# Splitting the softmax division, moving the key scale and taking a sigmoid for two sequences, in an attention and gated convolution kernel whose order is written out

## The chip, the cores and the metric

The kernel runs on one core of one Trainium2 chip. A core has five engines that each run their own list of instructions in order: TensorE (PE, matrix products, with its weight loads shown apart as PEld), VectorE (DVE), ScalarE (ACT, which evaluates functions such as exp from a table that has to be loaded), GpSimd (POOL) and SyncE (SP, which here only issues transfers). Semaphores make one engine wait for another. The metric is the device time of one execution in microseconds (us), the median of the runs shown.

## The reference

Eight sequences with eight heads of 64 channels and 576 positions each. Keys and values are averaged over blocks of 8 positions, so each head has 72 of them. After the attention comes a feed-forward part with a convolution along the sequence as its gate.

```python
k_p = k.reshape(B, H, 72, 8, D).mean(axis=3)
v_p = v.reshape(B, H, 72, 8, D).mean(axis=3)
scores = (1 / sqrt(64)) * q @ k_p^T
scores = scores - max(scores, axis=-1)
attn = exp(scores) / (sum(exp(scores)) + 1e-09)
x = (attn @ v_p), heads side by side          # (8, 576, 512)
h = relu(x @ w_in)                            # 512 -> 1024
conv_out[s] = sum over k of conv_w[k] * h[s + k - 1]   # 3 taps, per channel
out = (h * sigmoid(conv_out)) @ w_out         # 1024 -> 512, f32
```

## The kernel before, in words

**Tiles and stages.** The sequences go through attention in four groups of two: g0 is sequences 0 and 1, g3 is 6 and 7. A group has 1152 rows of queries, cut into tiles (g, t) of up to 128 rows, 37 tiles in all; a tile has all eight heads. A tile goes through these steps: scores on PE (`att_scores`, L563, its products at L582 and L595), the maximum of each head on DVE (`att_max`, L608), the subtraction of it (`att_shift`; on DVE at L620, for g0 on PE at L628), exp on ACT (`att_exp`, L646), the turn of the exponentials (on PE with a copy at L671 for g0 and g1, by a transposing DMA on SP at L666 for g2 and g3), the product with the values on PE (`att_values`, L682), which also gives the sum of the exponentials in one more column per head, the division (`att_divide`, L691), and the turn of the result x (PE with a copy at L722, or DMA at L706). The division is two DVE instructions behind one another: the reciprocal of the 8 sums of each row (L695) and one product of 128 x 512 that takes it broadcast along each head (L697). They are one operation in the graph, so nothing can come between them.

**The keys.** They are loaded either raw, and then pooled by a product with a matrix of ones (`clear_pool_matrix`, L341; `prep_k`, L401), or as heads, added up on DVE (`pool_pair`) and then picked apart by a product with parts of the identity (`build_pick`, L371; `turn_pair`, L441; `turn_keys`, L463). The sums are not divided by 8. Together with the reference's 1/8 this is made good by `scale=1/64` in exp (L646) alone.

**The feed-forward part** runs by sequence. `ffn_in` (PE, L727) fills 8 blocks of 128 channels x 576 positions, and `ffn_relu` (ACT, L736) takes them out of PSUM with a scale of 0.5. The gate is worked out in halves of four blocks, (b, f4), in one of two ways. Ten of the sixteen are convolved on PE (`ffn_conv`, L889) with diagonal matrices; a tanh on ACT (`ffn_tanh`, L914) takes the result out of PSUM; every second block has its two halves of 64 partitions swapped, so it goes to a buffer `tg`; `ffn_gate` adds 1 on DVE, to the unswapped blocks in one instruction (L925) and to the swapped ones in two that also swap back (L927); `ffn_times` (L935) multiplies with h. The other six, named in `TAPS` ((4,1), (5,0), (5,1), (6,0), (6,1), (7,0)), are done by taps: one tap on ACT (L862), two on DVE (L864), tanh on ACT (L869), and then `ffn_tap_gate` adds 1 (L875) and multiplies with h (L876). Since sigmoid(y) = (1 + tanh(y/2))/2, the 0.5 of relu is the outer half. `ffn_out` (PE, L943) is the last product; its result is copied out of PSUM by ACT or DVE (L954) to a buffer `osb`, for the last group to a "late" buffer (the memory of the query buffers `qp`), and stored (L966).

**What sets the order.** Every step is put into a graph by `add` (in `add_att` L1193, `add_ffn` L1246, `add_out` L1334) with its engine or a choice of two, its predecessors and the ring buffers that it takes. Three tables written out in the class `Graph` then decide everything: `ORDER` (1034 entries: the number of a step times two, plus one for the second of its two engines; -1 is a `fill`, a matmul without use on a scratch tile, L399, of which there are 17), `FORMS` (which of two shapes the scores take) and `PLACES` (which buffer or PSUM slot each step gets). An engine runs its steps in this order. Large loads are issued on POOL's queue, raw loads, transposing DMAs and most stores on SP's, some late stores on ACT's.

Of the kernel before, what the change touches and what calls it, by code (L numbers as in the profile page):

```python
# [9 lines left out]
BF16 = mybir.dt.bfloat16  # L10
AX = mybir.AxisListType
OP = mybir.AluOpType
# [21 lines left out]
class Graph:  # L34
# [35 lines left out]
    ORDER = (  # L70
# [107 lines left out]
def kernel(  # L178
# [23 lines left out]
    KW = 2 * Sp  # L202
    SLOTS = 24
    NJ = 5
    KP = NJ * P

    groups = [[0, 1], [2, 3], [4, 5], [6, 7]]
    where = {b: (g, i) for g, bs in enumerate(groups) for i, b in enumerate(bs)}
# [50 lines left out]
    graph = Graph(rings)  # L259
    add = graph.add  # L260

    def shift_by_dve(g, t):
        return (g, t) not in Graph.SHIFT_PE

# [1152 lines left out]
```

## Time and profile before

| what | value |
|---|---|
| runs | 217.02, 217.79, 217.13 us; median 217.13 |
| profiled execution | 216.5 us from its first to its last instruction |
| busy | PE 201.9, DVE 193.2, ACT 162.7, POOL 41.5 us |
| mean granted TensorE clock | 0.992 |
| transfers | HBM read 32.52 MB, written 9.44 MB |

The profile is of one execution. Its page gives each engine's busy time, the same in 40 equal slices (a digit is a tenth), the chain of work that ended last, followed back from the end, and the costliest groups of instructions: line, engine, operation, output <- input with shapes, count | busy us, mean ns of one | idle time of the engine just before them and what ended it. The trace behind it can be asked for single stretches and for the instructions in order of time: start, duration, engine, line, operation; a row with "x2" joins two that follow one another.

### The profile page before, as it was taken

The page shows a single profiled execution, that of the slowest core. Times are in us where ns is not written, and L with a number is a line of the kernel's source. Part 1 is how long each engine was busy: PE and PEld are TensorE (multiplying, and loading weights), DVE is VectorE, ACT ScalarE, POOL GpSimd, SP SyncE. Part 2 cuts the span into 40 slices and gives each one's busy share as a digit, 9 for nine tenths or more (in the row PEclk, how much of TensorE's full clock was granted, in tenths as well). Part 3 has the DMA queues.
Part 4 walks back from the last instruction along what each step waited for, and adds up shares of the span by engine and source line. Part 5 has one row for each costly group of instructions (what it writes and reads, how often), then busy time and mean ns, then how long its engine had stood idle before and what let it go on. Part 6 is the DMA issues. An engine that isn't in the chain of part 4 may idle for free.

```text
span 216.5 us, 6617 instructions
## 1 busy us (share of the span) xinstructions
PE 201.9 (93%) x2753; PEld 137.0 (63%) x2753; DVE 193.2 (89%) x334; ACT 162.7 (75%) x278; POOL 41.5 (19%) x78
## 2 busy tenths in 40 slices
PE   7599999969999999999999899989999999999992
PEld 3557778855788776766776675665656666654451
DVE  7598989999999999999999799999899999998621
ACT  2548885896998887787497594878979999997420
POOL 8644330050052101000000030002201210370000
PEclk9799999999999999999999999999999999999999
DMA  6999999999999999969687634576347745602685
GB/s 210 227 207 209 206 207 208 210 205 206 207 205 206 154 153 179 158 164 165 131 111 100 136 74 89 58 156 148 78 104 153 158 100 123 145 0 51 169 242 171
DMA packets 48833, 33.46 MB, mean 155 GB/s; under 512 B 28300, under 2 KB 43812, under 8 KB 48804
## 3 DMA queue, kind: packets, MB, share of 16 engines
q0 software_dynamic: 15216, 15.40, 43.5%
q1 hardware_dynamic: 32512, 16.13, 36.6%
q10 hardware_dynamic: 1076, 1.52, 2.5%
q8 instruction: 21, 0.34, 0.7%
q14 instruction: 8, 0.07, 0.1%
HBM read 32.52 MB, written 9.44 MB: 194 GB/s over the span
## 4 chain that ended last, share of the span: by engine, by line
PE 45%; DVE 34%; issue 6%; ACT 6%; DMA 5%; SPq 2%; DVEq 0%
PE psum L943 20%; PE psum L727 16%; DVE negm L608 7%; DVE x L697 6%; DVE sd L620 4%; DVE gT L935 4%; DMA hT<-in_k_dram 3%; DVE v L486 3%; DVE gT L927 3%; PE psum L889 2%; DMA out_dram<-osb 2%; DVE r L695 2%; PE psum L682 2%; ACT e L646 2%; DVE gT L925 1%
## 5 line engine op out<-in xcount | busy, mean ns | idle before, releaser
L727 PE MATMUL psum<-xT,w_in_sb 128*128 128x288 bf16 x512 | 74.1, 286 | 2.2 <-DMA xT<-x 1.1
L943 PE MATMUL psum<-w_out_sb,gT 128*128 128x512 bf16 (+1 forms) x296 | 69.5, 374 | 0.7 <-DVE gT L935 0.6
L727 PEld LDWEIGHTS <-w_in_sb 128*128 128x128 bf16 x512 | 47.9, 98 | 19.1 <-issue 2.0
L736 ACT ACTIVATE hT<-psum 128x576 bf16<-128x576 f32 x64 | 40.3, 650 | 14.0 <-PE psum L727 13.4
L943 PEld LDWEIGHTS <-gT 128*128 128x128 bf16 x296 | 27.3, 98 | 26.5 <-issue 0.9
L864 DVE SCALAR_TENSOR_TENSOR tg<-hT,convw,tg 128x576 f32<-128x576 bf16 x48 | 37.6, 815 | 0.5
L608 DVE TENSOR_REDUCE negm<-psum 128x8 f32<-128x576 f32 (+2 forms) x37 | 27.5, 752 | 2.3 <-PE psum L582 1.6
L697 DVE TENSOR_TENSOR x<-psum,r 128x512 bf16<-128x512 f32 (+1 forms) x37 | 25.6, 691 | 1.4
L811 POOL COPY hT<-hT 128x126 bf16<-128x126 bf16 x16 | 7.5, 467 | 97.6 <-ACT hT L736 80.1
L620 DVE TENSOR_TENSOR sd<-psum,negm 128x576 f32<-128x576 f32 x27 | 20.2, 753 | 0.5
L682 PE MATMUL psum<-vm,eT 128*128 128x130 bf16 (+5 forms) x240 | 18.9, 222 | 1.1 <-DVE x L697 0.7
L646 ACT ACTIVATE e<-sd 128x576 bf16<-128x576 f32 x27 | 18.2, 685 | 1.3 <-DVE sd L620 1.1
L954 ACT COPY osb<-psum 128x512 f32<-128x512 f32 x27 | 15.7, 585 | 4.4 <-PE psum L943 4.2
L889 PE MATMUL psum<-hT,dw 64*64 64x288 bf16 (+2 forms) x608 | 18.7, 261 | 0.1
L682 PEld LDWEIGHTS <-eT 128*128 128x128 bf16 (+1 forms) x240 | 15.3, 100 | 5.4 <-DMA eT<-e 1.2
L862 ACT ACTIVATE tg<-hT,convw 128x576 f32<-128x576 bf16 x24 | 18.1, 772 | 0.1
L889 PEld LDWEIGHTS <-dw 64*64 64x64 bf16 x608 | 14.8, 107 | 4.6 <-issue 3.7
L869 ACT ACTIVATE gT<-tg 128x576 bf16<-128x576 f32 x24 | 16.3, 683 | 0.7 <-DVE tg L864 0.5
L914 ACT ACTIVATE gT<-psum 128x576 bf16<-128x576 f32 x20 | 12.9, 651 | 3.9 <-PE psum L889 2.7
L914 ACT ACTIVATE tg<-psum 128x576 bf16<-128x576 f32 x20 | 13.0, 652 | 2.6 <-PE psum L889 1.4
L935 DVE TENSOR_TENSOR gT<-gT,hT 128x2304 bf16<-128x2304 bf16 x10 | 13.5, 1352 | 0.1
L486 DVE TENSOR_TENSOR v<-v 128x1280 bf16<-128x1280 bf16 (+2 forms) x24 | 13.0, 540 | 0.2
(84 smaller groups left out, 234.2 us busy)
## 6 DMA issues: line engine op xcount, KB each, us to landing
out_dram<-osb SPq DMA_DIRECT2D x54, 128.0 KB, 2.4
v<-in_v_dram POOLq DMA_DIRECT2D x8, 512.0 KB, 13.1
qp<-in_q_dram POOLq DMA_DIRECT2D x7, 576.0 KB, 14.4
kk<-in_k_dram POOLq DMA_DIRECT2D x3, 1152.0 KB, 14.6
out_dram<-qp ACTq DMA_DIRECT2D x10, 128.0 KB, 2.7
hT<-in_k_dram SPq DMA_DIRECT2D x2, 576.0 KB, 5.0
w_in_sb<-in_moe_w_in_dram POOLq DMA_DIRECT2D x2, 512.0 KB, 14.2
w_out_sb<-in_moe_w_out_dram POOLq DMA_DIRECT2D x1, 1024.0 KB, 24.7
```

Source lines behind the costliest of these rows:

```text
L608: nc.vector.tensor_reduce(out=a["m"][0:rows], in_=a["s"][0:rows, :, 0:2 * KW].rearrange("p a (h s) -> p a h s", s=Sp), axis=AX.X, op=OP.ma ...
L620: nc.vector.tensor_tensor(out=a["d"][0:rows], in0=a["s"][0:rows, :, 0:2 * KW].rearrange("p a (h s) -> p a h s", s=Sp), in1=a["m"][0:rows]. ...
L646: nc.scalar.activation(out=dst, in_=src, func=ACT.Exp, scale=1.0 / (POOL * 8.0),)
L682: nc.tensor.matmul(out=a["o"][lo:hi, h // 4, (h % 4) * (D + 1):(h % 4 + x1 - x0) * (D + 1)], lhsT=a["eT"][:, j, lo:hi], rhs=buf("vm", b)[: ...
L697: nc.vector.tensor_tensor(out=a["x"][0:rows].rearrange("p (a h d) -> p a h d", a=2, d=D), in0=ov[:, :, :, 0:D], in1=r[0:rows].unsqueeze(3) ...
L727: nc.tensor.matmul(out=banks(ps)[:, j, 0:SC], lhsT=w_in_block(dc, fb), rhs=buf("xT", g)[:, dc, i * S + j * SC:i * S + (j + 1) * SC], start ...
L736: nc.scalar.activation(out=h_of(b)[:, fb].rearrange("p (a s) -> p a s", a=2), in_=banks(ps)[:, :, 0:SC], func=ACT.Relu, scale=0.5,)
L864: nc.vector.scalar_tensor_tensor(out=acc, in0=h, scalar=w, in1=acc, op0=OP.mult, op1=OP.add)
L889: nc.tensor.matmul(out=banks(pss[r ^ c])[c * D:(c + 1) * D, j, lo:hi], lhsT=dw[r * D:(r + 1) * D, tap * n_fb + fb, :], rhs=hT[r * D:(r + 1 ...
L914: nc.scalar.activation(out=t.rearrange("p (a s) -> p a s", a=2), in_=banks(ps)[:, :, 0:SC], func=ACT.Tanh, scale=0.5,)
L935: nc.vector.tensor_tensor(out=gate, in0=gate, in1=h_of(b)[:, four], op=OP.mult)
L943: nc.tensor.matmul(out=bank(ps)[0:rows, columns], lhsT=buf("gT", g)[:, fb, t * P:t * P + rows], rhs=w_out_sb[:, fb, columns], start=(fb == 0),
```

## The change

It has five parts.

1. The division is two steps of the graph, `att_invert` (the reciprocal, on DVE) and `att_divide`, which has a choice: the product on DVE as before, or eight activations on ACT of 128 x 64 each, with the reciprocal as scale. In the new order 4 of the 37 tiles are divided on ACT: (2, 5), (2, 6), (3, 1) and (3, 7). Of the others, 19 have the product right behind the reciprocal on DVE, and 14 have something else between them.
2. The scale 1/64 is in the keys: in the pooling matrix, and in `ident_k`, a scaled copy of the identity (one more DVE instruction). exp has no scale.
3. For (6, 0), (6, 1), (7, 0) and (7, 1), listed in `SIG`, relu has scale 1 and the gate is a sigmoid instead of a tanh, so the "+1" falls away: three instructions of L875's kind and one of L925's; the two swapping instructions of (7, 1) are plain copies. In these and all other halves by taps the product with h is a step of its own, `ffn_times`. All exponentials stand ahead of the first sigmoid, and ACT loads one more table there.
4. The "late" output buffers wait for the query turns of sequences 4 to 7, where before they waited for those of 7 alone.
5. `ORDER` (1097 entries, 40 fills), `FORMS` and `PLACES` are new. 12 fills, where 14 were, stand ahead of the first other matmul, and 28, where 3 were, later. Some copies go to the other engine: DVE has three more copies to `osb`, two fewer of x, two more small and one more large of keys; one more copy of the late outputs stands ahead of DVE's last gate.

`EIGHT` is empty, so the branches on it never run. The diff, cut to its core:

```diff
 class Graph:
+    EIGHT = ()
+    SIG = ((6, 0), (6, 1), (7, 0), (7, 1))
-    ORDER = (0, 10, 12, 24, 16, -1, 4, 44, -1, 28, 8, -1, 36, ...)
+    ORDER = (0, 12, 10, 24, 16, 4, 44, 28, 8, 36, 14, 32, 46, ...)
...
+    KSCALE = 1.0 / (POOL * 8.0)
...
     def clear_pool_matrix():
-        nc.vector.memset(pm[0:TB, :, 0:Sp], 1.0)
+        nc.vector.memset(pm[0:TB, :, 0:Sp], KSCALE)
...
     def build_pick():
+        nc.vector.tensor_scalar(out=ident_k, in0=ident, scalar1=KSCALE, scalar2=None, op0=OP.mult)
...
     def att_exp(g, t):
...
             func=ACT.Exp,
-            scale=1.0 / (POOL * 8.0),
         )
...
-    def att_divide(g, t):
+    def att_invert(g, t):
+        nc.vector.reciprocal(out=buf("r", g, t)[0:rows_of(g, t)], in_=att_heads(g, t)[:, :, :, D])
+
+    def att_divide(g, t, engine):
         a, rows = att[g, t], rows_of(g, t)
-        ov = a["o"][0:rows, :, 0:4 * (D + 1)].rearrange("p a (h d) -> p a h d", d=D + 1)
-        r = buf("r", g, t)
-        nc.vector.reciprocal(out=r[0:rows], in_=ov[:, :, :, D])
+        ov, r = att_heads(g, t), buf("r", g, t)
         a["x"] = buf("x", g, t)
+        if engine == "ACT":
+            for n in range(H):
+                nc.scalar.activation(
+                    out=a["x"][0:rows, n * D:(n + 1) * D],
+                    in_=ov[:, n // 4, n % 4, 0:D],
+                    func=ACT.Identity,
+                    scale=r[0:rows, n // 4, n % 4:n % 4 + 1],
+                )
+            return
         nc.vector.tensor_tensor(
...
     def ffn_relu(b, fb, ps):
...
-            scale=0.5,
+            scale=1.0 if (b, fb // 4) in Graph.SIG else 0.5,
...
+    def squash(b, fb):
+        return ACT.Sigmoid if (b, fb // 4) in Graph.SIG else ACT.Tanh
...
     def ffn_tap_gate(b, f4):
...
         nc.vector.tensor_scalar(out=gate, in0=gate, scalar1=1.0, scalar2=None, op0=OP.add)
-        nc.vector.tensor_tensor(out=gate, in0=gate, in1=h_of(b)[:, four], op=OP.mult)
...
     def ffn_gate(b, f4):
...
+        if (b, f4) in Graph.SIG:
+            for r in range(2):
+                nc.vector.tensor_copy(out=gate[r * D:(r + 1) * D, 1], in_=tg[(1 - r) * D:(2 - r) * D])
+            return
...
-        o = add(dve(0.2, 0.69), key, lambda: att_divide(g, t), after=[o], uses=[x, rr, big])
+        o = add({"DVE": 0.115}, key, lambda: att_invert(g, t), after=[o], uses=[rr, big])
+        o = add({"DVE": 0.61, "ACT": 0.82}, key, None, after=[o], uses=[x, rr, big])
+        o.emit = lambda o=o: att_divide(g, t, o.engine)
...
-            gated = add(dve(0.78, 1.39), w, lambda f4=f4: ffn_tap_gate(b, f4), after=tanh, uses=[htok[b], gtok[g]])
+            need = tanh
+            if (b, f4) not in Graph.SIG:
+                need = [add(dve(0.78), w, lambda f4=f4: ffn_tap_gate(b, f4), after=tanh, uses=[gtok[g]])]
+            gated = add(dve(1.39), w, lambda f4=f4: ffn_times(b, f4), after=need, uses=[htok[b], gtok[g]])
...
-            osb, free = (token("late", g, t), qdone[7, 0]) if g == 3 else (token("osb", g, t), [])
+            osb, free = (token("late", g, t), [x for n in range(4, B) for x in qdone[n, 0]]) if g == 3 else (token("osb", g, t), [])
...
+    late = [o for part, o in squashed if part in Graph.SIG]
+    for o in late:
+        for e in exps:
+            e.next.append((o, True))
+            o.left += 1
```

More of the change, by code (lines that the diff above doesn't have):

```diff
@@ L640, in att_exp @@
         e = a["e"] = buf("e", g, t)
+        if by_head(g, t):
+            for n in range(H):
+                r, k = n // 4, n % 4
+                at = (k // 2 * 4 + r * 2 + k % 2 if a["by_rows"] else n) * Sp
+                nc.scalar.activation(
+                    out=e[0:rows, at:at + Sp],
+                    in_=a["s"][0:rows, r, k * Sp:(k + 1) * Sp],
+                    func=ACT.Exp,
+                    bias=a["m"][0:rows, r, k:k + 1],
+                )
+            return
         src = a["d"][0:rows].rearrange("p a h s -> p a (h s)") if shift_by_dve(g, t) else a["s"][0:rows, :, 0:2 * KW]
@@ L868, in ffn_tap_tanh @@
         gate = buf("gT", g)[:, fb, i * S:(i + 1) * S].rearrange("p (a s) -> p a s", a=2)
-        nc.scalar.activation(out=gate, in_=acc_of(b, fb, ps), func=ACT.Tanh, scale=0.5)
+        nc.scalar.activation(out=gate, in_=acc_of(b, fb, ps), func=squash(b, fb), scale=0.5)
     def ffn_tap_gate(b, f4):
         g, i = where[b]
-        four = slice(4 * f4, 4 * f4 + 4)
-        gate = buf("gT", g)[:, four, i * S:(i + 1) * S]
+        gate = buf("gT", g)[:, 4 * f4:4 * f4 + 4, i * S:(i + 1) * S]
         nc.vector.tensor_scalar(out=gate, in0=gate, scalar1=1.0, scalar2=None, op0=OP.add)
-        nc.vector.tensor_tensor(out=gate, in0=gate, in1=h_of(b)[:, four], op=OP.mult)
     def ffn_conv(b, f2, pss):
@@ L1209, in add_att @@
         o = add(dve(0.75), key, lambda: att_max(g, t), after=[o], uses=[ng, s])
-        if shift_by_dve(g, t):
+        if by_head(g, t):
+            o = add({"ACT": 0.9}, key, lambda: att_exp(g, t), after=[o], uses=[e, s, ng, lim])
+            exps.append(o)
+        elif shift_by_dve(g, t):
             sd = token("sd", g, t)
@@ L1325, in add_ffn @@
                                                    uses=[cb] + (tg if fb % 2 and tg else [gtok[g]])))
+                squashed.append(((b, f4), tanh[f4][-1]))
             if f2 % 2 and cross:
[L1327 removed]
+                need = tanh[f4]
+                if (b, f4) not in Graph.SIG:
+                    need = [add(dve(0.78), w + 6 * f2 + Graph.GATE, lambda f4=f4: ffn_tap_gate(b, f4), after=tanh[f4], uses=[gtok[g]])]
+                gated = add(dve(1.39), w + 6 * f2 + Graph.GATE, lambda f4=f4: ffn_times(b, f4), after=need, uses=[htok[b], gtok[g]])
                 gdone.setdefault(b, []).append(gated)
```

26 lines of the change are left out of this document (19 added, 7 removed), and 142 rows, old and new, of tables (ORDER, PLACES).

## The prediction

> **What bounds the kernel now.** I read the page's busy totals and its slices first, to see which engines could be the bound and whether that changes on the way.
>
> ```profile
> PE 201.9 (93%) x2753; PEld 137.0 (63%) x2753; DVE 193.2 (89%) x334; ACT 162.7 (75%) x278; POOL 41.5 (19%) x78
> ...
> PE   7599999969999999999999899989999999999992
> ...
> DVE  7598989999999999999999799999899999998621
> ACT  2548885896998887787497594878979999997420
> ```
>
> TensorE (PE) and VectorE (DVE) are both near full through the middle, ScalarE (ACT) only in the last third.  Next, the chain of work that ended last:
>
> ```profile
> PE 45%; DVE 34%; issue 6%; ACT 6%; DMA 5%; SPq 2%; DVEq 0%
> ```
>
> Two engines share the path, so I asked where each rules, with a table of long stretches (columns: length, then busy time of PE, PE's weight loads, DVE, ACT and POOL, clock, DMA share, GB/s) and one of stretches of 6 us:
>
> ```profile
> 24.00:150.00 126.00, 120.03 (x1982) 87.45 (x1982) 120.93 (x209) 99.19 (x171) 17.40 (x29) 1.00 0.95 159
> 151.30:198.20 46.90, 46.90 (x354) 28.20 (x353) 44.76 (x61) 43.77 (x75) 10.29 (x20) 1.00 0.48 106
> 12.00:72.00 60.00, 55.78 (x1033) 42.68 (x1033) 56.74 (x105) 48.88 (x84) 14.32 (x20) 1.00 1.23 207
> ```
>
> ```profile
> 6.00:12.00 6.00, 4.03 (x84) 3.81 (x88) 3.25 (x13) 3.21 (x6) 4.27 (x10) 0.72 1.19 213
> ...
> 114.00:120.00 6.00, 4.77 (x103) 3.34 (x91) 5.88 (x12) 4.15 (x7) 0.00 (x0) 1.00 0.81 112
> 120.00:126.00 6.00, 5.98 (x91) 4.67 (x92) 4.47 (x10) 4.65 (x8) 0.52 (x2) 1.00 0.49 105
> ```
>
> Up to 150 us PE and DVE wait for one another in turn: PE is idle for 126 − 120.03 = 6.0 us, DVE for 5.1. Since attention alternates between them (max, shift and divide on DVE between three PE steps), what DVE saves there lets PE start sooner, up to PE's 6.0 us. From 151.3 on PE never stops, so there a shorter DVE gives nothing by itself: PE ends earlier only by what it brought along. The end shows it:
>
> ```profile
> 198.30 0.76 DVE L875 TENSOR_SCALAR gT<-gT 128x2304 bf16<-128x2304 bf16 x1 [0.89 <-ACT gT L869]
> 199.10 1.36 DVE L876 TENSOR_TENSOR gT<-gT,hT 128x2304 bf16<-128x2304 bf16 x1
> 200.38 0.45 DVE L925 TENSOR_SCALAR gT<-gT 128x1152 bf16<-128x1152 bf16 x1
> 200.84 0.92 DVE L927 TENSOR_SCALAR gT<-tg 64x1152 bf16<-64x1152 bf16 x2
> 201.80 1.36 DVE L935 TENSOR_TENSOR gT<-gT,hT 128x2304 bf16<-128x2304 bf16 x1
> ...
> 212.28 0.42 DVE L954 COPY qp<-psum 128x256 f32<-128x256 f32 x1 [0.46 <-PE psum L943]
> ```
>
> ```profile
> 199.03 13.21 PE L943 MATMUL psum<-w_out_sb,gT 128*128 128x512 bf16 x68
> ```
>
> The last gate is done at 203.16; PE streams the output product without a hole until 212.24, 68 matmuls in 13.21 us.
>
> **The change part by part.** Counts are from both programs' instruction orders, durations from these groups:
>
> ```profile
> L697 DVE TENSOR_TENSOR x<-psum,r 128x512 bf16<-128x512 f32 x35 | 24.2, 692 | 1.3
> ...
> L954 ACT COPY osb<-psum 128x512 f32<-128x512 f32 x27 | 15.7, 585 | 4.4 <-PE psum L943 4.2
> ...
> L875 DVE TENSOR_SCALAR gT<-gT 128x2304 bf16<-128x2304 bf16 x6 | 4.6, 772 | 0.9 <-ACT gT L869 0.9
> ...
> L954 DVE COPY qp<-psum 128x512 f32<-128x512 f32 x3 | 2.1, 689 | 6.0 <-PE psum L943 6.0
> ...
> L722 DVE COPY xT<-psum 128x512 bf16<-128x512 bf16 x4 | 1.6, 415 | 0.0
> ...
> L479 ACT CAST kT<-psum 128x576 bf16<-128x576 f32 x2 | 1.2, 642 | 0.2 <-PE psum L468 0.2
> ...
> L431 ACT CAST kT<-psum 64x288 bf16<-64x288 f32 x2 | 0.8, 394 | 0.0
> ...
> L431 DVE CAST kT<-psum 64x144 bf16<-64x144 f32 x2 | 0.6, 312 | 2.6 <-PE psum L406 2.6
> L431 ACT CAST kT<-psum 64x144 bf16<-64x144 f32 x2 | 0.5, 270 | 1.1 <-DVE kT L431 1.1
> ```
>
> *DVE, by durations, up to the last gate.* Off: four divides 4 × 0.69 = 2.77; the "+1" of three sigmoid gates by taps 3 × 0.77 = 2.31; the "+1" of gate (7, 1) 0.45 (its two swapped halves become plain copies of the same shape, which I leave at 0.46); two turned copies of x 2 × 0.415 = 0.83. On: three output copies that were ACT's 3 × 0.69 = 2.07, one more output copy that now stands ahead of the last gate 0.69, two small kT casts 2 × 0.31 = 0.62, one kT copy of 128 x 576 that DVE did not do before (between the 0.31 cast and ACT's 0.64 I take 0.6, bounds 0.3 to 0.8), one eT copy 0.4, the scaled identity 0.15. Sum: −6.36 + 4.53 = −1.8 us.
>
> *DVE, by neighbours.* The split lets other work stand between reciprocal and product.
>
> ```profile
> 143.79 0.20 DVE L695 RECIPROCAL r<-psum 128x8 f32<-128x8 f32 x1
> 144.02 0.69 DVE L697 TENSOR_TENSOR x<-psum,r 128x512 bf16<-128x512 f32 x1
> 144.63 0.81 DVE L864 SCALAR_TENSOR_TENSOR tg<-hT,convw,tg 128x576 f32<-128x576 bf16 x1
> ```
>
> The product, which needs the reciprocal, starts 0.03 after its end; the tap behind it, which needs neither, 0.08 before the product's end. A dependent neighbour so costs 0.11 us. Over all of DVE's list (divides, taps, gates, pooling) such neighbours fall from 74 to 62: 12 × 0.11 = −1.3 (bounds 0 and −1.5). DVE in all: −3.1 us. By position: the new order has 1 to 1.5 us *more* DVE work ahead of sequence 0's gates (at 47 us), is even near 88, 1.5 ahead near 107, 2.5 near 145, 3.1 at the last gate.
>
> [...]
>
> *ACT.* Four tiles are divided by 8 activations of 128 x 64 each. The trace has no 64-column one; from 270 ns at 144 columns and 394 at 288 a line falls to 0.20 us at 64, a scale by pointer may add 0.1, and neighbours overlap.
>
> ```profile
> 44.83 1.09 ACT L458 CAST kT<-psum 64x288 bf16<-64x288 f32 x3
> ```
>
> Here three casts of 0.39 take 1.09, so 0.35 each. I take 0.22 each, 1.8 us a tile; bounds 0.1 (0.8 a tile, if all but the columns overlapped) and 0.37 (3.0). One more table load stands ahead of the first sigmoid:
>
> ```profile
> 0.81 1.28 ACT L1062 ACT_TABLE_LOAD   x1 [0.81 <-PEq L1403]
> ...
> 2.10 0.30 ACT L1062 CAST gT<-ident 128x128 f32<-128x128 bf16 x1
> ```
>
> 1.28 us, and the next operation 0.01 after it. Together 4 × 1.8 + 1.28 = 8.5 on; off about 3 (three output copies of 0.585, the kT copies, two late output copies, less two copies of x). ACT +5.5 us. From 24 to 150 us it is idle for 126 − 99.2 = 26.8 us, which hide what falls there. From there to the last tanh it has 46.9 − 43.77 = 3.1 us, into which go the load and one of the divided tiles, less a copy: +2.7.
>
> *PE.* The real matmuls are the same. Fills go from 17 to 40: 12 instead of 14 ahead of the first real matmul, 28 instead of 3 spread over the first 70 us.
>
> ```profile
> 1.23 4.57 PE L399 MATMUL psum<-gT 128*128 128x448 bf16 x14 [1.23 <-DVE gT L1052]
> ...
> 12.15 0.36 PE L399 MATMUL psum<-gT 128*128 128x448 bf16 x1
> 12.35 0.70 PE L595 MATMUL psum<-kT,qT 128*128 128x144 bf16 x4
> ```
>
> At full clock one occupies PE for 0.20 (12.15 to 12.35), early ones 4.57 / 14 = 0.33. 25 × 0.20 = 5.0 us against PE's 4.2 idle in 12 to 72. I price it at nothing, since 4.2 and the 2.0 of 6 to 12 us are more than 5.0, and a fill that falls into a wait costs nothing; without that cover it is up to 5.0. The clock was 1.00 in that stretch already, so they can win nothing there.
>
> *The rest at nothing*: the scale in the pooling matrix and the identity (same operations, other constant, an exponent without a scale has the same operands); the last output buffers wait for the query turns of sequences 4 to 7, long past; SP and POOL issue the same transfers, moved by a few us, with DMA load at 0.5 after 120.
>
> *Sum.* DVE's lead at 145, 2.5 us, is what PE can bring into its closed stretch; some of it is lost where PE waits for DMA or ACT instead, so I keep 2.1. The profiled execution's 216.5 goes to 214.4. The runs' median is 217.13, 0.6 above its span, so **215.0**, with 213.9 to 216.0 as its own range.
>
> **The rivals.** *C, full gain*: all 3.1 us come through and part of a DVE hole goes, too:
>
> ```profile
> 119.41 1.23 SPq L666
> ...
> 120.69 0.58 SPq L966
> ...
> 121.33 2.41 DMA out_dram<-osb
> 123.74 0.19 DVE r L695
> ```
>
> DVE's 1.5 us of 120 to 126 hang on SP's queue and a store; a new order may fall otherwise. 217.1 − 3.1 − 0.5 = **213.5**. Against it: PE's 46.9 of 46.9.
>
> *D, placing apart gives nothing* (the change does not do what it says): DVE −1.8 instead of −3.1, so 2.1 × 1.8 / 3.1 = 1.2, **215.9**.
>
> *B, ACT becomes the late bound*: 2.7 of its 3.1 us are used up. If the small activations take 0.37, 1.2 us more come in that stage, ACT is 0.8 over its limit, relu evicts PSUM late and PE stops for between that and 0.8 + 1.28 (the load, if PE's buffers fill meanwhile); with 1.4 of it the gain shrinks to 0.7, **216.4**. [...]
>
> *A, slower*: the fills lie on PE's path. Place: the first 70 us, where DVE has only 60 − 56.74 = 3.3 us of slack and the new order gives it 1 to 1.5 us more ahead of the first gates. Each fill ahead of scores for which DVE waits delays DVE by 0.20. It decides once over half of the 25 do so; with 20, +4.0 − 2.1 = +1.9, **219.0**. For it: the idle time of PE is split into many short waits. Against it: 4.2 us of idle PE there.
>
> **How the numbers follow.** Chances: forecast 0.36, C 0.17, D 0.05, B 0.18, A 0.24. A measurement of this kernel tells 0.5% from no change, 1.09 us: below 216.05 is faster, above 218.2 slower. Forecast, C and D are faster: 0.58. B is 0.15 the same and 0.03 beyond, with A 0.27 slower. The range goes from 212.8 (C with −1.5 for the neighbours and the whole hole) to 219.3 (A with 21 or 22 fills), leaving out about 0.1 on each side.
>
> **What would show it.** Right: DVE busy near 191, fewer dependent neighbours; the last gate about 3 us earlier; PE still without holes after 150 and its last stretch starting 2 us earlier; ACT near 168, the eight small activations at 1.8 us a tile. Wrong: DVE idle over 3.3 us in 12 to 72 with PE as releaser (A); PE holes released by relu's eviction after 160 (B); a reciprocal's follower gaining nothing (D); PE idle up to 150 still 6 us although DVE is shorter, which would mean that something else than DVE sets the attention's pace.

## The result, and the profile after

The changed kernel takes 219.53 us (median of 7 runs, 218.88 to 220.13); the kernel before, run beside it, 217.37 (7 runs, 217.02 to 218.61). The ratio is 1.0088, interval 1.0062 to 1.0113: slower, by about 1.9 us, where 215.0 and a gain were forecast. The profiled execution of after took 218.99 us with a span of 217.3, so 1.7 us lie outside its span. The ratios leave out disturbed executions (of the kernels below, two of e11's ten, one of e12's twelve and five of e13's nine, the profiled one among them), so a ratio can be lower than its median suggests.

The page of the kernel after, engines' busy time and the chain of work that ended last:

```profile
PE 203.4 (94%) x2842; PEld 137.2 (63%) x2842; DVE 192.2 (88%) x333; ACT 167.6 (77%) x305; POOL 39.7 (18%) x78
...
PE 64%; DVE 14%; DMA 8%; issue 5%; ACT 5%; SPq 1%; DVEq 0%
```

DVE has less to do, as meant (192.2 for 193.2), ACT 4.9 us more, PE 1.5 more; the path has moved from DVE (34% before) to PE (64%). The same stretches as before, of the kernel after (columns as in the prediction):

```profile
12.00:72.00 60.00, 56.99 (x1076) 42.52 (x1080) 55.12 (x105) 45.42 (x78) 14.39 (x24) 1.00 1.19 200
24.00:150.00 126.00, 122.52 (x2064) 89.66 (x2062) 119.06 (x204) 104.25 (x192) 16.67 (x33) 1.00 0.92 159
...
151.30:198.20 46.90, 45.78 (x357) 27.38 (x356) 43.37 (x60) 44.79 (x81) 9.66 (x20) 1.00 0.48 105
```

Two things stand out. In 12 to 72 us DVE is idle for 4.9 us where it was idle for 3.3, and most of it ends with a result of PE (3.8 us): the sign that the prediction gave for rival A. And the stretch from 151.3, in which PE never stopped, now has 1.1 us of holes. Cut finer, first before, then after:

```profile
42.00:48.00 6.00, 4.54 (x113) 3.91 (x102) 5.85 (x9) 5.96 (x12) 3.11 (x4) 1.00 1.24 207
48.00:54.00 6.00, 5.26 (x89) 3.06 (x87) 5.93 (x10) 4.22 (x8) 0.00 (x0) 1.00 1.24 206
...
150.00:174.00 24.00, 24.00 (x188) 14.42 (x187) 23.16 (x36) 22.12 (x39) 3.48 (x8) 1.00 0.58 125
174.00:204.00 30.00, 30.00 (x219) 17.36 (x217) 28.19 (x36) 26.53 (x46) 6.81 (x12) 1.00 0.37 85
```

```profile
42.00:48.00 6.00, 4.60 (x135) 3.25 (x120) 4.74 (x9) 4.59 (x10) 1.67 (x2) 1.00 1.24 207
48.00:54.00 6.00, 5.25 (x138) 3.38 (x137) 5.61 (x8) 4.16 (x6) 0.69 (x2) 1.00 1.24 206
...
150.00:174.00 24.00, 23.96 (x190) 14.55 (x189) 23.34 (x34) 22.79 (x50) 2.62 (x8) 1.00 0.63 132
174.00:204.00 30.00, 28.68 (x201) 15.90 (x200) 26.82 (x35) 26.63 (x44) 7.04 (x12) 1.00 0.37 84
```

So there are two places: 42 to 54 us, where DVE loses 1.4 us, and 174 to 204, where PE and DVE are busy for 1.3 to 1.4 us less each.

**The early place.** PE's timeline, after and then before, the rows that end an idle time put down to "issue" (bracket: idle time ahead of the row):

```profile
44.37 0.32 PE L925 MATMUL psum<-hT,dw 64*64 64x63 bf16 x6 [1.15 <-issue]
...
50.29 0.32 PE L532 MATMUL psum<-ident,qp 64*64 64x64 bf16 x15 [0.75 <-issue]
```

```profile
45.15 0.22 PE L657 MATMUL psum<-ident,e 128*128 128x128 bf16 x1 [0.29 <-issue]
```

"Issue" means that no semaphore that the profile shows was waited for. Counted in PE's instruction list, the two instructions of after are numbers 1471 and 1727, 256 apart, and the one of before is its number 1471 too, though it is another operation. The kernel after has 88 more PE instructions ahead of the operation that stands there: 14 fills of two instructions each, and smaller shapes of scores and of query turns (`FORMS` holds both) for 60. The queue that carries instructions moved 22 packets, 0.36 MB (before 21, 0.34), some 16 KB each. The reading (theory F in the expectations): PE's program arrives in blocks of 256 instructions, and a kernel that uses a block up before the next has come runs dry.

The traces keep the time of each packet of that queue. Borders are PE's numbers 1471, 1727 and every 256 on either side; times are in us.

| kernel | PE passes a border | the next packet starts | it has landed | PE passes the next border | PE stood still |
|---|---|---|---|---|---|
| after | 38.91 | 42.04 | 42.99 | 44.37 | 1.15 |
| after | 44.37 | 48.02 | 48.96 | 50.29 | 0.75 |
| before | 39.42 | 42.88 | 43.85 | 45.15 | 0.29 |
| e2 | 38.83 | 42.10 | 43.05 | 44.40 | 1.25 |
| e9 | 38.58 | 41.84 | 42.80 | 44.12 | 1.75 |
| e14 | 40.06 | 42.88 | 43.85 | 45.56 | no stop |
| e3 | 43.03 | 45.18 | 46.15 | 48.97 | no stop |

In the 17 traces there are 24 stops of this kind, and in each of them PE goes on 1.2 to 1.5 us behind the landing of a packet. Theory F says besides that the blocks come at times that do not depend on the kernel's order, and in that it is wrong: the packet follows PE's passing of the border before. In e3 PE passes it 4.1 us later than in after, and the packet starts 3.1 us later. After used up the 256 instructions of its two blocks in 4.3 and 5.2 us, before those of its one in 5.4, and the next block could be used only 5.5 to 5.9 us behind the border. So what counts is not the 88 as such, but how fast PE goes through the block that it is in; more and smaller instructions put other work into the block. PE of after so stands still for 1.15 and 0.75 us; the gates of sequence 0 end 0.73 and 1.53 us later than before, the third 2.70. The 0.73 is not the stop's: that gate ends before the stop does, and is 0.84 and 0.86 us late in e1 and e14 as well, which have no stop there.

**The late place.** ACT's timeline of the kernel after at the first sigmoid, then PE's, then DVE's:

```profile
174.91 0.64 ACT L994 COPY osb<-psum 128x512 f32<-128x512 f32 x1
175.56 1.28 ACT L907 ACT_TABLE_LOAD   x1
176.86 0.68 ACT L907 ACTIVATE gT<-tg 128x576 bf16<-128x576 f32 x1
```

```profile
179.51 3.32 PE L762 MATMUL psum<-xT,w_in_sb 128*128 128x288 bf16 x24 [0.59 <-ACT hT L771]
...
203.99 8.83 PE L983 MATMUL psum<-w_out_sb,gT 128*128 128x512 bf16 x48 [0.24 <-DVE gT L975]
```

```profile
180.16 0.82 DVE L899 SCALAR_TENSOR_TENSOR tg<-hT,convw,tg 128x576 f32<-128x576 bf16 x1 [1.37 <-ACT tg L897]
...
186.38 1.74 DVE L899 SCALAR_TENSOR_TENSOR tg<-hT,convw,tg 128x576 f32<-128x576 bf16 x2 [0.91 <-ACT tg L897]
...
202.57 1.36 DVE L975 TENSOR_TENSOR gT<-gT,hT 128x2304 bf16<-128x2304 bf16 x1
```

ACT comes to the load without a gap, and PE (relu, L771) and DVE (the tap on ACT, L897) wait behind it. The last gate is done at 203.93 (203.16 before), and the end follows 13.4 us behind it (13.3 before). This is the prediction's rival B (theory L in the expectations).

### The profile page after: what moved, and what is told of

The parts are those of the page before. It is cut to its first block, busy times and chain, and to the rows that moved or that the text cites. A ratio compares the mean times of both kernels' runs of the same rounds, so it can differ in the third digit from the quotient of the medians.

```text
span 217.3 us, 6857 instructions
## 1 busy us (share of the span) xinstructions
PE 203.4 (94%) x2842; PEld 137.2 (63%) x2842; DVE 192.2 (88%) x333; ACT 167.6 (77%) x305; POOL 39.7 (18%) x78
## 4 chain that ended last, share of the span: by engine, by line
PE 64%; DVE 14%; DMA 8%; issue 5%; ACT 5%; SPq 1%; DVEq 0%
PE psum L762 21%; PE psum L983 18%; PE psum L925 6%; DVE tg L899 6%; PE psum L704 5%; DMA eT<-e 4%; DMA hT<-in_k_dram 3%; PE psum L411 2%; DVE gT L975 2%; PE psum L679 2%; PE psum L749 2%; PE psum L607 2%; PE psum L594 1%; PE psum L532 1%; PE psum L640 1%
## 5 line engine op out<-in xcount | busy, mean ns | idle before, releaser
L762 PE MATMUL psum<-xT,w_in_sb 128*128 128x288 bf16 x512 | 71.4, 286 | 0.8 <-ACT hT L771 0.6
L983 PE MATMUL psum<-w_out_sb,gT 128*128 128x512 bf16 (+1 forms) x296 | 68.6, 373 | 1.0 <-DVE sd L632 0.3
L771 ACT ACTIVATE hT<-psum 128x576 bf16<-128x576 f32 x64 | 40.9, 659 | 8.1 <-PE psum L762 6.5
L732 DVE TENSOR_TENSOR x<-psum,r 128x512 bf16<-128x512 f32 (+1 forms) x33 | 22.3, 685 | 0.7
L975 DVE TENSOR_TENSOR gT<-gT,hT 128x2304 bf16<-128x2304 bf16 x16 | 21.7, 1359 | 0.4
L925 PE MATMUL psum<-hT,dw 64*64 64x288 bf16 (+2 forms) x608 | 19.0, 261 | 1.5 <-issue 1.1
L925 PEld LDWEIGHTS <-dw 64*64 64x64 bf16 x608 | 15.1, 107 | 6.4 <-issue 5.3
L897 ACT ACTIVATE tg<-hT,convw 128x576 f32<-128x576 bf16 x24 | 18.6, 787 | 0.3
L411 PE MATMUL psum<-gT 128*128 128x448 bf16 x40 | 13.3, 421 | 3.1 <-DVE gT L1092 2.8
L994 ACT COPY osb<-psum 128x512 f32<-128x512 f32 x24 | 14.2, 598 | 1.9 <-PE psum L983 1.2
## 6 DMA issues: line engine op xcount, KB each, us to landing
v<-in_v_dram POOLq DMA_DIRECT2D x8, 512.0 KB, 13.4
```

Source lines behind the costliest of these rows:

```text
L732: nc.vector.tensor_tensor(out=a["x"][0:rows].rearrange("p (a h d) -> p a h d", a=2, d=D), in0=ov[:, :, :, 0:D], in1=r[0:rows].unsqueeze(3) ...
L762: nc.tensor.matmul(out=banks(ps)[:, j, 0:SC], lhsT=w_in_block(dc, fb), rhs=buf("xT", g)[:, dc, i * S + j * SC:i * S + (j + 1) * SC], start ...
L771: nc.scalar.activation(out=h_of(b)[:, fb].rearrange("p (a s) -> p a s", a=2), in_=banks(ps)[:, :, 0:SC], func=ACT.Relu, scale=1.0 if (b, f ...
L897: nc.scalar.activation(out=acc, in_=h, func=ACT.Identity, scale=w)
L925: nc.tensor.matmul(out=banks(pss[r ^ c])[c * D:(c + 1) * D, j, lo:hi], lhsT=dw[r * D:(r + 1) * D, tap * n_fb + fb, :], rhs=hT[r * D:(r + 1 ...
L975: nc.vector.tensor_tensor(out=gate, in0=gate, in1=h_of(b)[:, four], op=OP.mult)
```

## The experiments

Fifteen runs; unless said otherwise an edit is to the kernel after. Ratios are to the kernel before, run beside them. In the expectations some numbers go back to a lag of 3.4 us of after behind before between 50 and 115 us. That lag was summed over PE's matmul records; gates and relus, which are single instructions, give 1.5 to 2.7 there, and those are used below.

### Fewer instructions, or less work, for PE (F)

**e1, without the 28 late fills:**

```diff
-fill(t)
+fill(t) if n < 12 else None
```

> The changed kernel without the 28 late fills (the first 12 stay), all else as it was; 56 PE instructions fewer. Against the kernel before, the real work of PE in the changed kernel is 2.0 us late at 24 to 40 us, 4.9 at 48, 3.4 from 50 to 115, level at 146, 1.5 ahead at 166 to 180 and 0.8 late at the end. Theory A (a fill costs the 0.2 us that it occupies PE): the 2.0 of 24 to 40 and about 1.5 of the step at 43 to 50 go, the lag from 50 to 115 falls to about 0.5, and the time from 219.5 to 217 or less. Theory F (PE stops at its instructions 1471 and 1727 because the next block of its program has not come, which happens at a time that does not depend on the kernel's order): 38 instructions fewer of the 88 that the changed kernel has more ahead of 1471, so the stop of 1.15 us at 43 shrinks by less than half, the lag from 50 to 115 falls to about 2.3, and the time to about 218.5. Theory L (only the late stage matters, where ACT is full from 172 to 192): 219.5, no change over 0.4.

218.77 us, ratio 1.0034 (1.0007 to 1.0061): 0.5% gained. The long stops are gone (two of 0.29 us are left, at 50.82 and 89.42); gate 2 is 0.11 us ahead of before (1.53 behind in after). But the ten executions differ by their granted clock: five with 0.995 or more took 217.48 to 218.61, five with 0.984 to 0.989 took 218.92 to 219.72. Stretches of the profiled one (clock 0.988):

```profile
12.00:15.00 3.00, 2.33 (x34) 1.73 (x33) 3.00 (x12) 1.30 (x2) 2.08 (x4) 0.90 1.21 206
15.00:18.00 3.00, 2.72 (x67) 1.58 (x69) 2.35 (x5) 1.82 (x4) 0.00 (x0) 0.54 1.21 207
```

The clock is 0.54 there, where after has 1.00. So the fills do two things: they use up PE's program, and with them the clock stays up (0.996 or more in all seven executions of after).

**e2, the late fills 16 columns wide in place of 448:** the same instructions, nearly none of the time (three in a row at 10.6 us take 0.22 us, in after 0.73).

```diff
-rhs=blank
+rhs=blank[:, 0:n]      # n = 448 for the first 12, then 16
```

> The 28 late fills have 16 columns instead of 448: the same number of PE instructions, almost none of the occupied time. Theory A (occupied time): like the run without them, 217 or a little over, lag from 50 to 115 about 0.7. Theory F (number of instructions ahead of the block border): the stop at PE's instruction 1471 stays at 1 us or grows, since PE gets there earlier, the one at 1727 too; the lag from 50 to 115 stays at 3 or more and the time at 219 or more. Theory L: 219.5.

219.96 us, 1.0091 (1.0059 to 1.0124): nothing gained against after's 1.0088. PE's timeline and the clock of e2:

```profile
44.40 0.32 PE L925 MATMUL psum<-hT,dw 64*64 64x63 bf16 x6 [1.25 <-issue]
...
50.32 0.32 PE L532 MATMUL psum<-ident,qp 64*64 64x64 bf16 x15 [0.76 <-issue]
```

```profile
51.00:54.00 3.00, 2.78 (x8) 0.94 (x7) 2.18 (x4) 0.80 (x1) 0.00 (x0) 0.50 1.25 207
```

The stops stand at the same two instructions within 0.03 us of where they stood in after. So the stops are not the price of the fills' work; their number is what remained. (e2 also pays for a lower clock, 0.5 here, so e1 against e2 isn't a clean pair; the place of the stops is.)

**e3, six entries of `FORMS`, all of them turns of queries, back to the larger shape** (216 PE instructions fewer, all fills kept):

```diff
-FORMS[8, 11, 15, 16, 17, 19] = 1
+FORMS[8, 11, 15, 16, 17, 19] = 0
```

> All fills as in the changed kernel; six transposes of queries take the form of half the instructions (18 matmuls of 128x64 weights instead of 36 of 64x64), which costs PE about 0.2 us more for each of them. Four stand ahead of PE's instruction 1471: 144 instructions fewer there. Theory F: the stops by issue at 43 and 49 us fall from 1.15 and 0.75 to under 0.3 together, the lag from 50 to 115 from 3.4 to under 2.3, the time to 218.3 or less. Theory A: nothing is won, 0.8 to 1.2 us more PE time ahead of 55 us, 219.5 to 220.5. Theory L: 219.5.

219.1 us, 1.007 (1.004 to 1.01). Both stops are gone: in 42 to 54 us PE is busy for 11.56 us, where after has 9.85. But gate 1 is 2.19 us behind before (after 0.73): the larger shapes cost about 1.4 us ahead of 43 us. With fewer instructions for the same work PE takes 5.9 us over the block and finds the next one there, so the stops hang on the count once more; the net gain was nearly nothing.

**e9, the kernel before with 42 thin fills more** behind its three late ones:

```diff
-fill(t)
+[fill(t, 448)] + [fill(t, 16) for _ in range(14 if n >= 14 else 0)]
```

> The kernel before with 42 thin fills of 16 columns (84 PE instructions) put behind its three late fills, at 12 to 16 us. Theory F (PE's program comes in blocks with borders at PE instructions 1471 and 1727, and the blocks come at about 44.5 and 50.4 us whatever the order): PE now reaches 1471 some 2 us of work earlier and stops there, in the convolution, for 0.8 to 1.5 us, and again at 1727; 0.8 to 1.8 us slower than before (ratio 1.004 to 1.008). Theory A (occupied time): 42 x 0.03 = 1.3 us at most, mostly in waits at 12 to 16 us, and no stop at 44: ratio under 1.003.

220.6 us, 1.0113 (1.0051 to 1.0175): slower than before by about what the change itself costs. PE's timeline, and the clock behind the stop:

```profile
44.12 0.29 PE L889 MATMUL psum<-hT,dw 64*64 64x224 bf16 x4 [1.75 <-issue]
```

```profile
45.00:48.00 3.00, 3.00 (x41) 2.71 (x39) 2.91 (x6) 2.96 (x8) 2.37 (x3) 0.50 1.25 210
```

It is PE's instruction number 1471 again, though a different operation, and one more stop, of 0.50 us, ends at 22.95, three blocks ahead. Gates 2 to 5 are 1.2 to 1.3 us late; the low clock behind the stop may have a share in that. The old order with more PE instructions has the new order's stop: with the times of the packets, this mirror settles that PE waits for its program.

### The table load and ACT's last third (L)

**e4, tanh in place of sigmoid** for all halves. It leaves out the "+1" that a tanh needs, so the gates of sequences 6 and 7 have wrong values; the instructions are otherwise the same:

```diff
-return ACT.Sigmoid if (b, fb // 4) in Graph.SIG else ACT.Tanh
+return ACT.Tanh
```

> Tanh in place of sigmoid, without the +1, so no second table is loaded (1.28 us at 175.6); the gates of sequences 6 and 7 are left wrong by that. Theory L (ACT is the bound from 172 to 204, where PE loses 2.2 us against the kernel before): PE's holes of 0.59 at 178.9 and 0.28 in 180 to 186 go, the last gate comes 1 to 1.3 us earlier, 218.3 to 218.5. Theories A and F alone: within 0.4 of 219.5, since DVE's chain of taps then sets the end. If the time outside the span (1.7 us here) holds the preparation of a second table, it shrinks, too.

218.42 us, 1.0029 (1.0006 to 1.0053): 0.6%, 1.3 us gained, the length of the load.

**e7, the load 8 us earlier,** by a sigmoid of 128 x 8 on a scratch tile, ahead of an output copy:

```diff
-for o in graph.order():
+for n, o in enumerate(graph.order()):
+    if n == 904:
+        nc.scalar.activation(out=sig0, in_=ident[:, 0:8], func=ACT.Sigmoid)
```

> The changed kernel with a sigmoid of 128 x 8 on a scratch tile ahead of ACT's copy at 167.8, where ACT waits 0.92 us for PE: the table load moves there from 175.6. Theory L: the wait takes most of the load, 0.5 to 0.9 us faster than the changed kernel (ratio to the kernel before 1.005 to 1.006); DVE's holes of 1.37 and 0.91 at 180 and 186 shrink. Theories A and F alone: no change over 0.4.

218.88 us, 1.0049 (1.0025 to 1.0073): 0.85 us gained, though the interval overlaps with after's (1.0062 to 1.0113). ACT of e7:

```profile
167.45 1.28 ACT L1453 ACT_TABLE_LOAD   x1
168.74 0.21 ACT L1453 ACTIVATE sig<-ident 128x8 bf16<-128x8 bf16 x1
```

and e7's last stretch, against after's 28.68 of PE and 26.82 of DVE:

```profile
174.00:204.00 30.00, 29.54 (x209) 16.65 (x208) 28.04 (x37) 26.09 (x44) 6.84 (x12) 1.00 0.38 87
```

The same work with the load elsewhere closes most of PE's and DVE's holes. The length of the late stage says it more sharply than the medians. From the eleventh of the sixteen products with h (done at 171.06 us in after) to the last, after takes 32.87 us, e2 32.87 and e6 32.86; e4, without a second table, 31.45; e7 31.66, and e11, e12 and e14 below, with the same early load, 31.64 to 31.66. So most of what the load costs hangs on its place.

**e10, e7 with three output copies on ACT, as before:**

```diff
-ORDER 1470, 1704, 1446
+ORDER 1471, 1705, 1447
```

> The run with the early table load, and three output copies of 177 to 188 us (tiles (2, 3), (2, 5), (2, 0)) on ACT again, as in the kernel before: DVE loses 3 x 0.6 us in the late stage, ACT gets 3 x 0.5. If DVE's own work is what counts at the end (DVE has no hole from 194.6 to 203.9): 0.5 to 1.2 us faster than the run with the early load (ratio 1.000 to 1.003). If ACT is the bound there (L): 0.5 to 1.2 slower (1.007 to 1.010). If it is the chain from one to the other: no change.

220.15 us, 1.0089 (1.0053 to 1.0125), against e7's 1.0049. The intervals overlap, and the profiled execution is 0.8 us behind e7's at the first gate already, so the size is left open. The late stage takes 32.70 us, 1.04 more than in e7: work given back to ACT does not help, although DVE has less.

**e5, tile (3, 7) divided on DVE:**

```diff
-ORDER 1907
+ORDER 1906
```

> The changed kernel with the tile (3, 7) divided on DVE at the same place of the order: ACT loses the eight activations of 1.75 us at 171.5, DVE gets a product of 0.69. Theory L (the late stage is a chain of taps between ACT and DVE, in which 1 us of ACT is 1 us of the end): 0.7 to 1.2 us faster than the changed kernel, 218.3 to 218.8 where that is 219.5 (ratio to the kernel before 1.004 to 1.006). Theory B as forecast (only the sum of ACT's work counts, and 2.7 of 3.1 us idle were used): the same direction. Theory D (DVE sets the end): 0.3 to 0.7 slower.

219.14 us, 1.0078 (1.0052 to 1.0105): within 0.1% of after. Nothing: what ACT is spared, DVE pays.

### Placing apart

**e6, the reciprocal back in front of its product** on DVE, all else as in after:

```diff
+i.emit = lambda o=o: att_invert(g, t) if o.engine == "ACT" else None
+o.emit = lambda o=o: (att_invert(g, t) if o.engine == "DVE" else None, att_divide(g, t, o.engine))
```

> The changed kernel with every reciprocal put back right ahead of its product on DVE (the four of the tiles divided on ACT stay where they are); 14 pairs become neighbours again. If a dependent neighbour costs 0.11 us: 1.5 us more on DVE by the last gate, of which 0.5 to 1.5 reaches the end. If placing apart gives nothing: within 0.4 of 219.5. A rival of both: reciprocals that stand early free nothing, but one that stands in front of other work makes that wait for values from PE; then adjacent is faster by up to 0.5.

220.51 us, 1.0155 (1.0103 to 1.0207): 0.7%, 1.5 us slower than after, from four executions and with intervals that overlap. The traces carry it: up to the last gate DVE is busy for 0.95 us more than in after, and its gaps under 60 ns add up to 0.62 us more, together 1.6 us for 14 pairs, as the prediction's 0.11 us a pair gave. The last gate is done 1.05 us later, so DVE's time does reach the end, for the most part.

### Together

**e8, e1 with e5 and e7:**

```diff
-fill(t)
+fill(t) if n < 12 else None
-ORDER 1907
+ORDER 1906
+    if n == 904:
+        nc.scalar.activation(out=sig0, in_=ident[:, 0:8], func=ACT.Sigmoid)
```

> The changed kernel without its 28 late fills, with the tile (3, 7) divided on DVE and with the table load at 167.8. If the early loss (F, about 1.2 us by the run without fills) and the late one (L, 1 to 2 us) add up: 216.8 to 217.3, ratio to the kernel before 0.994 to 0.999. If one hides the other (the late chain starts from the same DMA or PE event whatever happens ahead of it): not under 1.002.

218.66 us (217.42 to 219.64), 1.0051 (1.0023 to 1.0078). Less than the sum of its parts, and scattered as e1 is (clocks of 0.978 to 1.000). The late stage, which starts here at 169.35 us, takes 32.90 in spite of the early load. It tells little.

**e11, e7 with only the first 21 fills, and two query turns in the larger shape:**

```diff
-fill(t)
+fill(t) if n < 21 else None
-FORMS[15, 16] = 1
+FORMS[15, 16] = 0
```

> The run with the early table load, with the first 21 fills alone (19 fewer) and two of the query transposes ahead of 43 us in the form of half the instructions: 92 PE instructions fewer ahead of 1471, about as many as the kernel before has there, with the fills that stand at 11 to 15 us kept. Theory F: no stop at 44 or 50, gates of sequence 0 done 1 us earlier, 0.8 to 1.2 us faster than the run with the early load: ratio 1.000 to 1.001. If the lost time of 43 to 50 us is not F's: 1.004 to 1.006.

218.06 us, 0.9981 (0.994 to 1.0023): 0.7% better than e7, with gate 2 at +0.26 and no stop in 42 to 54 us. A stop of 0.74 us ends at 92.02, at the border six blocks on, so F isn't quite gone from this kernel.

**e0, the kernel before once more** with a profile:

> The kernel before once more, for its span beside its time and for how its trace varies: if the time outside the span is 1.7 us here as it is in the changed kernel, the profile shown of before (216.5) was of a run of about 218.2, 0.8 to 1.1 above the median.

218.35 us with a span of 216.7. So about 1.7 us lie outside before's span, as in after, and every gate stands within 0.25 us of the profile shown.

**e12, e11 again, to see how it scatters:**

> The run with fewer instructions and the early table load once more, in five rounds: 0.996 to 1.001 of the kernel before. If its gain of 0.7% over the early load was F's, it holds; if it was the scatter of that chip, 1.003 to 1.006.

217.24 us, 0.999 (0.996 to 1.002). Eight of the twelve executions took 215.97 to 217.40, three with a clock of 0.991 took 218.92 to 219.12. The profiled one is of the three:

```profile
42.00:54.00 12.00, 9.88 (x266) 6.67 (x264) 10.30 (x17) 8.66 (x15) 2.35 (x3) 0.86 1.24 207
```

PE passes both borders without a stop, and yet it is no busier than in after. The low clock, 0.72 in 48 to 54 us, is not all of it: in 42 to 48 us PE is busy for 4.80 of the 6 us at a clock of 1.00, and its longest wait there, 0.83 us, is for a copy of keys on ACT.

**e13, e11 with tiles (3, 1) and (3, 7) divided on DVE:**

```diff
-ORDER 1635, 1907
+ORDER 1634, 1906
```

> The same, with the tiles (3, 1) and (3, 7) divided on DVE as well: ACT has 3.5 us less between 149 and 174, where it is busy for 23.8 of 24 us in the run with fewer instructions, DVE 1.4 more. If the rest of DVE's saving is lost because ACT is the bound there: 0.5 to 1.5 us faster than that run (0.990 to 0.997 of the kernel before). If it is the chain of the last taps on DVE that sets the end: no change or up to 0.7 slower (0.998 to 1.004).

221.95 us (218.50 to 223.17), 1.0098 (1.0063 to 1.0132). DVE's and PE's timelines:

```profile
149.29 0.19 DVE L718 RECIPROCAL r<-psum 128x8 f32<-128x8 f32 x1
149.40 1.36 DVE L976 TENSOR_TENSOR gT<-gT,hT 128x2304 bf16<-128x2304 bf16 x1
150.68 0.45 DVE L966 TENSOR_SCALAR gT<-gT 128x1152 bf16<-128x1152 bf16 x1
151.15 0.92 DVE L968 TENSOR_SCALAR gT<-tg 64x1152 bf16<-64x1152 bf16 x2
152.10 1.36 DVE L976 TENSOR_TENSOR gT<-gT,hT 128x2304 bf16<-128x2304 bf16 x1
153.38 0.68 DVE L733 TENSOR_TENSOR x<-psum,r 128x512 bf16<-128x512 f32 x1
```

```profile
154.12 5.14 PE L984 MATMUL psum<-w_out_sb,gT 128*128 128x512 bf16 x16 [2.36 <-DVE x L733]
```

The product stands behind four gate instructions in DVE's queue; PE waits for it for 2.36 us, and its next 16 matmuls take 5.14 us (the same 16 in e14 3.83): the clock of 150 to 174 is 0.93. The product's place behind the gates is given by the order, and so is the same in all nine executions; how much of the lower clock is in the 1.0098 this one profile can't say. For (3, 1), then, the division on ACT isn't a saving of work, it is a way past DVE's queue. Whether one of the two alone would help on DVE was e5's question, for (3, 7): nothing.

**e14, e11 with fills 32 to 40 back,** which stand behind 50 us, to hold the clock:

```diff
-fill(t) if n < 21 else None
+fill(t) if n < 21 or n >= 31 else None
```

> The run with fewer instructions with the nine fills of 46 to 65 us back (fills 32 to 40; they stand behind PE's instruction 1471). In the runs without them the time falls into two sets: a granted clock of 0.994 to 1.000 with 216.0 to 217.4, and 0.991 with 218.9 to 219.1, whose profile shows a clock of 0.86 in 42 to 54 us. If the fills hold the clock there: only the first set, a median of 216.5 to 217.2, ratio 0.993 to 0.998. If the clock falls for another reason: two sets as before, ratio 0.996 to 1.002. By theory F alone the 14 instructions more ahead of 1727 could bring back a short stop at 50 us, 0.3 at most.

216.83 us (215.96 to 218.28, 12 executions), 0.9986 (0.9964 to 1.0008), all clocks 0.995 or more. Stretches of e14:

```profile
42.00:48.00 6.00, 5.74 (x162) 4.39 (x154) 5.86 (x11) 5.70 (x11) 2.35 (x3) 1.00 1.24 208
48.00:54.00 6.00, 5.54 (x140) 3.47 (x125) 5.90 (x9) 4.59 (x9) 0.00 (x0) 1.00 1.24 206
...
150.00:174.00 24.00, 23.96 (x188) 14.41 (x187) 23.22 (x35) 23.85 (x48) 2.40 (x8) 1.00 0.63 122
174.00:204.00 30.00, 29.55 (x206) 16.53 (x205) 26.95 (x35) 24.83 (x43) 6.82 (x12) 1.00 0.41 94
```

No stop, no lost clock, the late holes mostly closed: 1.0% better than after. It is the best version that was found, and its interval with before still includes 1.

## Why the prediction was wrong

**The step that failed** is the one on PE: "I price it at nothing, since 4.2 and the 2.0 of 6 to 12 us are more than 5.0, and a fill that falls into a wait costs nothing", and behind it "The clock was 1.00 in that stretch already, so they can win nothing there". Both halves are wrong, for one reason: a fill was counted only by the time that it occupies PE. It is also two of PE's instructions, and it also keeps PE from being idle. The sentence ahead of them, "The real matmuls are the same", is wrong as well: without the fills, before has 2736 matmuls and after 2802, since the new `FORMS` picks smaller shapes, and of the 88 instructions more these shapes are 60. With a new block of the program usable only 5.5 to 5.9 us behind the border before it, PE went through its blocks too fast and stopped for 1.15 and 0.75 us (e2, e3, e9 and the packets' times: shown). And without the fills the clock falls in some executions (e1: 0.984 to 0.989 in five of ten; e12: 0.991 in three of twelve; that it is the idle time which lowers it was only argued). Cost against before: about 1.4 us (e14 for e7, 0.6%, clock and stops together), 1.2 by e1.

The packets agree with the 256 between the stops at 1471 and 1727: after has 22 of 16 KB for 2842 matmuls and as many weight loads, one for 258 of these instructions, before 21 for 2753 and as many, one for 262. Crossing a border isn't free here: PE of after and e9 stops for 0.75 to 1.75 us, while transfers run at 204 to 209 GB/s (3 us around each stop). In after the packet starts 2.4 to 3.8 us behind PE's border up to 51 us, and at most 1.3 us behind from 97 to 119 us, where transfers run at 81 to 161 GB/s. For the most part that fits with these transfers delaying the blocks, but it was not tried.

**Rival A** was given 0.24 with its place (late fills, the first 70 us), its sign and 219.0 us. It had the place and the sign; its mechanism (0.20 us of occupied PE ahead of DVE's scores, per fill) does not show: e2 took the occupied time away, kept the stops and gained nothing. So place and sign came right for another reason.

**ACT.** "From there to the last tanh it has 3.1 us, into which go the load and one of the divided tiles, less a copy: +2.7" was right as a sum: eight activations took 1.74 us, where 1.8 was taken. (For the 0.1 of a scale by pointer, before has two groups of ACT at 128 x 576: L862, which reads one, takes 772 ns, L869, which reads none, 683.)

```profile
125.55 1.74 ACT L725 ACTIVATE x<-psum,r 128x64 bf16<-128x64 f32 x8
```

The load took 1.28, and the next operation came 0.02 behind its end. What was wrong is the conclusion that 2.7 into 3.1 costs nothing. The free 3.1 us are spread over 47 us, and the load is one piece of 1.28 at a place where PE and DVE both wait for ACT. It cost 1.3 us altogether (e4), 0.85 of it by its place (e7); by the length of the late stage 1.4 and 1.2. Rival B was so true beside A, not in its place.

**DVE by durations.** Forecast −1.8. Summed in the same way, over the durations of DVE's instructions up to the last gate, it is −1.6 (207.4 before, 205.9 after), so this term was nearly right. (The busy totals of the two pages, 193.2 and 192.2, count overlapping time once and run to the end.) Of the difference 0.16 is the large copy of keys (0.758, taken as 0.6); the four copies of parts of the identity that now read its scaled copy take 0.3 more; the swapped gates went from 485 to 537 ns each, the unswapped from 542 to 462, which leaves 0.2. Shorter products take some of that back.

```profile
L967 DVE TENSOR_SCALAR gT<-tg 64x1152 bf16<-64x1152 bf16 x18 | 9.7, 537 | 0.2
...
L965 DVE TENSOR_SCALAR gT<-gT 128x1152 bf16<-128x1152 bf16 x9 | 4.2, 462 | 0.0
...
L491 DVE CAST kT<-psum 128x576 bf16<-128x576 f32 x1 | 0.8, 758 | 0.2 <-PE psum L480 0.2
```

**DVE by neighbours.** Forecast −1.3. For the pairs this was right: e6 puts 14 of them back and costs 1.5 us by the medians, 1.6 by DVE's rows, so rival D falls. But against before the gain did not arrive on DVE. DVE's gaps under 60 ns, which stand for the most part between dependent neighbours (by the tiles' names 95 in before, 76 in after), fell from 104 to 91; the instructions that start before the one ahead has ended fell, too, from 199 to 194, since gaps of 60 to 250 ns, which are waits, rose from 18 to 31. Busy time and gaps under 60 ns together are 1.6 us less up to the last gate (2.3 in e14), where 3.1 were forecast. This is the second term that was mis-sized.

**The gain of 2.1.** It came, and went again. The two orders take the relus of a sequence in different turns, so the lag of after behind before is given as the median over a sequence's eight relus: +0.5 us for sequence 0, +1.7 for 1 and 3, +1.6 for 2 (up to 117 us), −0.2 and −0.1 for 4 and 5 (121 to 155 us), −0.6 and −0.9 for 6 and 7. So the early loss was made good by sequence 4. What did it was not taken apart: DVE had less to do, and the hole at 120 to 126, on which rival C counted, is shorter too, DVE being busy for 5.56 us there and 4.47 before. At the last gate, past the load, the lag is +0.8. In e14, with both losses treated, the last gate of the profiled execution is 1.5 us earlier than before's and the span 0.8 shorter; by the medians only 0.1% remains, 0.3 us.

**The median.** "0.6 above its span" was wrong: 1.7 to 1.8 us lie outside the span in the later profiled runs (2.0 in e12's). The profiled execution of before was about 0.8 slower than its median, which is why the spans differ by 0.8 and the medians by about 2.

**What stays open.** In e14 DVE's busy time and short gaps up to the last gate are 2.3 us less than before, and with both losses treated the kernel is not clearly faster. Candidates are ACT, which in e14 is busy for 23.85 of the 24 us from 150 to 174, and the stores at the end: behind its last gate e14 needs 14.1 us to the end, before 13.3, although PE's last 48 matmuls take 8.83 us in it as in after. Neither was settled. The edits that the prediction put at nothing beside these (the scale in the keys, the late buffers, SP's and POOL's issues) were not tried by themselves.

## What to carry to other kernels

Count an engine's instructions as well as its time: many small ones in a stage that runs close to full can make it wait for its own program (1.15 and 0.75 us in after), and the sign is an idle time put down to "issue" that falls on a border of 256 instructions, at the same number whatever the operation is (1471 in before, after and e9). What counts is how fast the engine goes through one such block, so the larger shape of an operation can be worth its time. Idle time that is spread thin can't take one long piece of work (here 3.1 us over 47, and a load of 1.28 that cost 1.3): price a table load by the queue that stands behind it at its place, and put it where nobody waits for that engine. Before a useless matmul is called free or useless, look at both what it delays and what clock is granted without it.

## What the runs showed of the hardware

- A gap of PE of 1.75 us was followed by a clock of 0.50 for three us (e9); one of 2.36 us by 0.93 over 24 us (e13). The low stretches in the clock records of e1, e2, e9, e12 and e13 each last 3.41 us at 0.50, as does one of before (8.23 to 11.64 us). In e1 the clock was 0.54 in 15 to 18 us, with PE busy for 2.72 of those 3 and for 2.33 of the 3 ahead of them. A gap alone doesn't decide it: after's 1.15 us left the clock at 1.00.
- PE's program comes in packets of 16 KB: in after 22, 0.36 MB, for 5684 matmuls and weight loads; its two stops, at 1471 and 1727, stand 256 instructions apart. In the 24 stops at a border PE went on 1.2 to 1.5 us behind the landing of a packet; in the first 50 us the packet itself started 1.9 to 4.3 us behind PE's passing of the border before.
- Eight ACT operations of 128 x 64 that read a scale per partition take 1.74 us in a row, 0.22 each, though the profile's mean of one is 332 ns: neighbours overlap.
